# A table in a pool of its own and a new step order in a spectral mixture-of-experts kernel

## The chip, the cores and the metric

The kernel runs on one core of a Trainium2 chip. The metric is the device time of one execution in microseconds (us); the time given for a kernel is the median of its runs. Five engines work side by side, each on its own queue in order: PE (TensorE, matmuls and transposes), DVE (VectorE), ACT (ScalarE), POOL (GpSimd) and SP (SyncE). DMAs are issued from the queues of SP, ACT and POOL.

## The reference

Only what decides the computation is kept:

```python
X = np.fft.rfft(x, axis=1)                     # x: 8 x 1856 x 256
Yr = Xr @ w_r - Xi @ w_i + b_r                 # Xr, Xi: real and imaginary part
Yi = Xr @ w_i + Xi @ w_r + b_i
Yr = np.sign(Yr) * np.maximum(np.abs(Yr) - lam, 0.0)      # Yi alike, lam = 0.01
y = np.fft.irfft(Y, n=x.shape[1], axis=1)      # 14848 rows of 256
g_idx = np.argmax(y @ w_group, axis=1)         # 4 groups
e_idx = np.argmax(yg @ w_expert[g], axis=1)    # 4 experts in the group: 16 in all
h = np.maximum(ye @ w1[g, e], 0.0)             # 256 -> 1024
out[rows] = (g_w * e_w)[:, None] * (h @ w2[g, e])   # 1024 -> 256; softmax weights of both picks
```

## The kernel before

The eight sequences are worked on as four pairs. For each pair the kernel makes a Fourier transform in two stages (1856 = 58 x 32), a complex linear map with a soft threshold, and the inverse in two stages; the rows go to `ys_d` in device memory. Logits are made from the same rows, routing on DVE picks an expert for each row, and a scatter on POOL writes the row's number and weight into that expert's list `lst`. The expert layers then gather rows through these lists. Weights, rows and hidden values are split into a high and a low fp32r half, so that each product is three matmuls.

From the first pair's second stage up to the first eight expert jobs (experts 0 to 3, 256 rows each) the order of all engines' work is written out by hand. `ORDER` is a string of 1434 letters; each letter calls the next step of one generator, and a step issues its instructions to one engine at that place (`manual_schedule`). No planner changes this order afterwards. Each engine works off its own instructions in order, and waits by semaphore for what the others make. After `ORDER` the remaining experts run in a loop over `jobs`.

The letters, with the lines of the profile. A step is named below by its letter and its number from 0; with 15 steps to a pair, k45 to k59 belong to the last pair:

| letter | line | engine | what one step does |
|---|---|---|---|
| c, d | 326, 330 | PE, DVE | first stage: four 64x512 matmuls; transpose of one half |
| e | 599 | PE | second stage: matmuls with the table `T`; one step feeds two f (the eighth of a pair one) |
| f, h | 606, 611 | ACT, DVE | high and low half of a bank: `xh`, `xl` |
| j, k | 617, 627 | ACT, PE | bias into `pw`; 12 matmuls of the linear map |
| m, n, o | 637, 637, 643 | ACT, ACT, DVE | two relus and their difference: the soft threshold |
| r, s | 657, 665 | PE, DVE | inverse, first stage, four r to a pair, after the pair's last o; s is its transpose, two to an r |
| v, w, x | 676, 688, 698 | PE, ACT, DVE | inverse, second stage, eight v to a pair; w copies `ysb` and every second w issues the 512 KB store to `ys_d`; x transposes into `yt` |
| G, H | 709, 718 | PE, DVE | logits of half a pair, after the x of four v; transpose into `L` |
| R | 154 to 232 | DVE, few ACT and PE | one operation of the routing; 33 to half a pair; among them the exponentials (162, ACT), the two bf16 matmuls (208, 210, PE) and `sloti` (227) |
| S | 240 | POOL | one scatter into `lst`, 16 to half a pair |
| l | 571, 576 | SP | load of 1 MB of x, or of an expert's w1 or w2, into one of two `xt` buffers; those of experts 2 and 3 wait for the last w issued |
| W, V | 740, 745 | ACT, DVE | high and low half of 512 columns of a weight |
| I, Z | 754, 761 | SP, POOL | load of lists `ent_a`, `ent_b`; their conversion to indices |
| F | 432 | POOL | an expert job's gather: two indirect DMAs of 128 rows into `xg` |
| T, X, Y | 779, 784, 788 | PE, ACT, DVE | transposes of `xg`; high and low half |
| U, A, B | 800, 808, 812 | PE, ACT, DVE | up projection, four U to a job; relu; low half |
| D, E, J, K | 824, 836, 843, 512 | PE, ACT, DVE, POOL | down projection, four D to a job; scaling; sum; store of 128 rows |
| L, M | 857, 866 | SP, POOL | the lists for the rest, and the first gather through them |

Three things set where waits can arise. `pa` has three PSUM buffers of two banks each, for c, e, r (two buffers to a step), v, G, T, D and the routing's two matmuls; `pw` has two, one to a k. A scatter waits for the fifth one before it to have landed (the first 64 for the third, and for a matmul of an earlier step). And the gathers F0 (lists a) need `xp2`, which is opened once the last o has been issued and the forward pools are closed:

```python
if c == "o" and done == NP * 15:
    fwd.close()
    xp2 = ctx.enter_context(tc.tile_pool(name="xp2", bufs=3, side="right"))
    early["mp"] = ph.enter_context(tc.tile_pool(name="mp", bufs=1))
```

`mp` holds X's and Y's results (`xth`, `xtl`), one job's at a time.

Of the kernel before, what the change touches and what calls it, by code (L numbers as in the profile page):

```python
# [34 lines left out]


ORDER = """
jejleffhlheekkfnhmojkfnhmojcfnhkmddjocfnhkmddjocfnhcmdkdjdodcfmhcndcdjdeddcdoeddekkfnhmojkfnhmojefnhkmojkfnhmjoefnhmkojk
fnhmjoefnhmeojkkfnhmjokfnhmjokfnhmjokfnhmjorfnhmkjssorfnhmkjssornmjokssrnmjoesscffhchdvldcxwxwkddddcnmcdljcddvldxvwdwkxw
xxwdocmnvdjvdwxcxwdlGdwovxxwxvwHwxvwxexwxReRffhwhwkxRRRRRRRGRfnhmRRjoRRRRkRHRRRRRRRkfnhmjoRRnkRmRjRoRRenRmSRRojefRfehSRh  # L40
RRkRRSRRRRRSRkRfRhnmRRSojRkfRRnhSmRRRjRkfSomhnojSRrnmojSRkssSRrmRRSnRojesSseffhSRkRRhSrfmShnksjSsorSfnhmesjSscSovddkwSxx
wSvfnhvwxmSxkwxwowxSjvfnhvSwxmvxwoGwSjSkHSxxwxwRvSwxRnvxwcwSxxRcwldwkdSmdjdxSRRRcmRRRGldSdRRRoRcRnRHcjdedlddeRfRRfhhcRRo
cdkdlddRRRRefnhmRRojkRRRRRefRSRnhkmRRRRjRSoRRRkfRnShmRojRSkfRnhRmRRSRjokRfRnhSmRRRRjRRkmSonSjoRRmeRnRRjSRefofhhSkRRRSrfm
hSnksjSsorfSnhmksjSsoSrmnojSkssSrnmSojeWsWSWseffhWShvWVWvxwVwSkxwxWxwSVWvVfVlmvxSwhwkxwxSnxwojVvfSVmGhwVnSlojvSxxwkxwHSw
xRRkRmSRRnRRojRSRvmRnRvxwSxewxjowefxfhwIhkRRRRRRRRRGRfRRmZhnRjoRRHkRRRRRkfRShmnRRSojRkRmSRRnRRRSRjoReSmRnRSjoeffShRhkSRR
RRRSRRRRkRSfRmnShojRSkmnSoSRmRnSRoRSrRRFRRssrSSsSTsXSYrSUsSsrASBSUWsWSsWUASWBvAVSWBUWxSWVWDVASVwBwvSxxDwSxwVvESVvxwFxwDx
wJwlDxKVVGEJKITHvXRRYRvwZxUxwRRwFxUAxwlBURARBFRURARBDARFRRBvRRRRDxwxwRDRERJRKDRRRTERXFJRYvRUwxWxKwURRARWBTAGRFWBWRRVWVWV
WSVWUHlSRRUVRSARRBDSARRXBTSYDRRSRURERSJRRDRARRSBURRRSRRRURASDBASBUVEFWVWJDVABWlRSWDVXVSYDVEJSVDSUESWJWVUAKVWBRTARKUWBRKU
RARBKDRABXTYDRRSVVUESJDASBUSUSABDSABSUEJSDXAYSTBUSUASBDASBUESJDASBUSDSAXBDKYEJKUKUABKLDABUEJKUABMDABDDEJDKDEJKDEJK
"""  # L50
# [1151 lines left out]
```

## Time and profile before

| | |
|---|---|
| time, median of 3 runs | 1126.11 us (1124.45 to 1127.98) |
| profiled execution | 1124.21 us, its span 1122.4 us |
| DVE busy | 663.9 us (59%) |
| ACT busy | 548.5 us (49%) |
| POOL, scatters (line 240) | 128, 1021 ns of work each |
| HBM read, written | 103.49 MB, 35.00 MB |

The span is cut by time in the rows that are shown below: `ORDER` covers about 16 to 473 us of it. A row of the timeline gives start, duration, engine, line, operation, tiles and number of merged instructions, and in brackets the idle time of the engine ahead of it and what ended that. Matmuls overlap in the pipeline, so that the time of a PE step is read from its start to the start of the next one, not from its duration. PEclk is the granted clock as a share of full speed.

### The profile page before, as it was taken

The numbers are of one execution on the slowest core, as the hardware profiler recorded it, in microseconds if no ns is written. First come the engines' busy times: TensorE is split into PE (matmuls) and PEld (weight loads), VectorE is DVE, ScalarE is ACT, GpSimd is POOL, SyncE is SP. The second block draws the span as 40 slices with busy tenths as digits, with TensorE's granted clock in tenths as the row PEclk, the third lists the DMA queues.
The fourth block names the chain that finished last, engine by engine and source line by source line (L and its number), as shares of the span: only waits on it lengthen the run. The fifth ranks groups of instructions, "written<-read, shape, count | busy, mean of one in ns | idle before, by whom it ended". The sixth has DMA issues, their size and how long they took to land. (4 is left out here: it accounts for less than half of the span.)

```text
span 1122.4 us, 19716 instructions
## 1 busy us (share of the span) xinstructions
PE 1096.3 (98%) x7282; PEld 892.9 (80%) x7282; DVE 663.9 (59%) x1453; ACT 548.5 (49%) x1234; POOL 403.7 (36%) x462
## 2 busy tenths in 40 slices
PE   8999999999998999999999999999999999999996
PEld 5686576677674689899999898888979889798785
DVE  4635777686877786366647554473554745454452
ACT  2565455545653454345546544473454635444352
POOL 3000014415447567643242343323433333333311
PEclk9999999999999999999999999999999999999999
DMA  9600610360510632414424245345424354245300
GB/s 381 183 1 1 223 79 2 128 175 1 164 64 11 219 122 67 131 51 135 173 63 156 97 171 195 117 142 225 137 76 157 122 211 166 79 169 196 112 23 24
DMA packets 42500, 138.88 MB, mean 124 GB/s; under 512 B 17462, under 2 KB 19772, under 8 KB 32034
## 3 DMA queue, kind: packets, MB, share of 16 engines
q1 hardware_dynamic: 21602, 89.22, 23.1%
q0 software_dynamic: 15904, 31.48, 9.0%
q10 hardware_dynamic: 4896, 16.91, 4.1%
q8 instruction: 58, 0.95, 0.4%
q14 instruction: 40, 0.33, 0.1%
HBM read 103.49 MB, written 35.00 MB: 123 GB/s over the span
## 5 line engine op out<-in xcount | busy, mean ns | idle before, releaser
L526 PE MATMUL py<-big,hh 128*128 128x512 f32 x824 | 294.1, 398 | 0.0
L465 PE MATMUL ph<-xth,big 128*128 128x384 f32 (+1 forms) x896 | 256.3, 362 | 0.7 <-ACT xth L452 0.7
L527 PE MATMUL py<-big,hl 128*128 128x256 f32 x824 | 230.6, 280 | 0.0
L240 POOL DMA_INDIRECT lst<-ent,sloti x128 | 130.7, 1021 | 250.9 <-DVE mx_g L156 140.0
L471 DVE SCALAR_TENSOR_TENSOR hl<-ph,hh 128x256 fp32r<-128x256 f32 x448 | 151.2, 379 | 65.7 <-ACT hh L469 61.5
L526 PEld LDWEIGHTS py<-big,hh 128*128 128x128 f32 x824 | 154.8, 188 | 34.7 <-issue 3.2
L465 PEld LDWEIGHTS ph<-xth,big 128*128 128x128 f32 x896 | 165.2, 188 | 19.8 <-issue 1.5
L469 ACT ACTIVATE hh<-ph 128x256 fp32r<-128x256 f32 x448 | 134.2, 352 | 70.4 <-PE ph L465 69.8
L465 PE MATMUL ph<-xtl,big 128*128 128x384 f32 (+1 forms) x448 | 162.2, 362 | 0.3 <-DVE xtl L453 0.3
L512 POOL DMA_INDIRECT out_dram<-yo,si_f x93 | 94.6, 1017 | 178.0 <-DVE yo L534 160.0
L527 PEld LDWEIGHTS py<-big,hl 128*128 128x128 f32 x824 | 155.1, 188 | 0.1
L432 POOL DMA_INDIRECT xg<-ys_d,gi_f x93 | 90.5, 973 | 179.1 <-PE pg L448 156.3
L534 DVE SCALAR_TENSOR_TENSOR yo<-py,ent_f,yo 128x256 f32<-128x256 f32 x93 | 45.0, 484 | 163.8 <-ACT yo L533 163.8
L533 ACT ACTIVATE yo<-py,ent_f 128x256 f32<-128x256 f32 x93 | 44.1, 475 | 190.0 <-PE py L527 190.0
L415 DVE TENSOR_TENSOR big<-xt,big 128x512 fp32r<-128x512 f32 x160 | 108.9, 680 | 0.0
L414 ACT CAST big<-xt 128x512 fp32r<-128x512 f32 x160 | 99.6, 622 | 0.0
L627 PE MATMUL pw<-wh,xh 128*128 128x512 f32 x240 | 98.5, 410 | 0.0
L627 PE MATMUL pw<-wl,xh 128*128 128x512 f32 x240 | 94.8, 395 | 0.0
L465 PEld LDWEIGHTS ph<-xtl,big 128*128 128x128 f32 x448 | 84.5, 189 | 8.2 <-DVE xtl L453 0.6
L611 DVE TENSOR_TENSOR xl<-bank,xh 128x512 fp32r<-128x512 f32 x60 | 40.8, 692 | 48.2 <-PE pw L627 30.3
L599 PEld LDWEIGHTS bank<-T,big 128*128 128x128 f32 x480 | 58.5, 196 | 10.0 <-issue 3.2
L606 ACT CAST xh<-bank 128x512 fp32r<-128x512 f32 x60 | 34.2, 587 | 65.8 <-PE pw L627 56.3
(197 smaller groups left out, 1639.9 us busy)
## 6 DMA issues: line engine op xcount, KB each, us to landing
xt<-in_w_dram SPq DMA_DIRECT2D x48, 1024.0 KB, 5.1
ys_d<-ysb ACTq DMA_DIRECT2D x32, 512.0 KB, 4.8
big<-in_w_dram SPq DMA_DIRECT2D x16, 1024.0 KB, 8.7
big<-in_x_dram SPq DMA_DIRECT2D x8, 1024.0 KB, 9.7
xt<-in_x_dram SPq DMA_DIRECT2D x8, 1024.0 KB, 7.5
lst<-ent,sloti POOLq DMA_INDIRECT x128, 3.0
lst<-zero SPq DMA_DIRECT2D x1, 1920.0 KB
xg<-ys_d,gi_f POOLq DMA_INDIRECT x93, 2.8
```

The source lines that it names most:

```text
L240: ins = nc.gpsimd.indirect_dma_start(out=lst, out_offset=bass.IndirectOffsetOnAxis(ap=sl_, axis=0), in_=en_, in_offset=None, bounds_check= ...
L414: nc.scalar.copy(out=wt[:, 2 * i, cs], in_=raws[i][:, cs])
L415: nc.vector.tensor_tensor(out=wt[:, 2 * i + 1, cs], in0=raws[i][:, cs], in1=wt[:, 2 * i, cs].bitcast(F32), op=ALU.subtract)
L432: ins = nc.gpsimd.indirect_dma_start(out=xg[:, c, :], out_offset=None, in_=ys_d[0:rows, :], in_offset=bass.IndirectOffsetOnAxis(ap=ids.gi[ ...
L465: nc.tensor.matmul(o[:, :n], lhsT=a_[:, ch, fs], rhs=b_[:, ch, 0:n], start=k == 0, stop=k == 5)
L469: nc.scalar.activation(out=hh[:, f, :m], in_=ov, func=AF.Relu)
L471: nc.vector.scalar_tensor_tensor(out=hl[:, f, :m], in0=ov, scalar=0.0, in1=hh[:, f, :m].bitcast(F32), op0=ALU.max, op1=ALU.subtract)
L512: ins = nc.gpsimd.indirect_dma_start(out=out, out_offset=bass.IndirectOffsetOnAxis(ap=ids.si[:, t:t + 1], axis=0), in_=ysb, in_offset=None ...
L526: nc.tensor.matmul(o, lhsT=hh[:, f, ts], rhs=w2b[:, :, f, :], start=f == 0, stop=f == 7, skip_group_check=True)
L527: nc.tensor.matmul(o[:, 0:D], lhsT=hl[:, f, ts], rhs=w2h[:, f, :], start=False, stop=f == 7, skip_group_check=True)
L599: nc.tensor.matmul(o.rearrange("p (j c) -> p j c", j=4)[:, :, m * 32:m * 32 + 32], lhsT=zys[pr][:, k, bt, :, kp], rhs=T[:, 2 * k + kp, :], ...
L627: ins = nc.tensor.matmul(y, lhsT=a_[:, c * 128:c * 128 + 128], rhs=w_[:, c // 2, c % 2].rearrange("p j e -> p (j e)"), start=False, stop=a ...
```

## The change

The table `T` of step e moves from the pool `cf`, which lives until the last o, into a pool `ct` on the right side of SBUF, which is closed once the last e (NP * 8 = 32 of them) has been issued. `xp2` and `mp` are opened there and then, `mp` on the right side too. So a gather F and the transposes T may stand ahead of the last o. The string `ORDER` is replaced: it has the same 1434 letters, each as often as before, in another order from about the 245th on. All matmuls, copies and DMAs are the same; the code after `ORDER` is too.

```diff
-cdkdlddRRRRefnhmRRojkRRRRRefRSRnhkmRRRRjRSoRRRkfRnShmRojRSkfRnhRmRRSRjokRfRnhSmRRRRjRRkmSonSjoRRmeRnRRjSRefofhhSkRRRSrfm
+cfRnRhcmdkdjlddRRkfomhnojknmojRRneRmRojeRfRfeRRhShkRRRRSRRRRRRkfRSnhmRRRojSRkfRRnhmRRSRjRRRkRfRmShoRnRSeRjomRnRrSRfojhks
...
-    T = cf.tile([128, K1, 128], F32, name="T")
+    table_t = ExitStack()
+    ct = table_t.enter_context(tc.tile_pool(name="ct", bufs=1, side="right"))
+    T = ct.tile([128, K1, 128], F32, name="T")
...
-        done = 0
+        done, turned = 0, 0
         for c in ORDER.replace("\n", ""):
             next(steps[c])
             done += c == "o"
+            turned += c == "e"
+            if c == "e" and turned == NP * 8:
+                table_t.close()
+                xp2 = ctx.enter_context(tc.tile_pool(name="xp2", bufs=3, side="right"))
+                early["mp"] = ph.enter_context(tc.tile_pool(name="mp", bufs=1, side="right"))
             if c == "o" and done == NP * 15:
                 fwd.close()
-                xp2 = ctx.enter_context(tc.tile_pool(name="xp2", bufs=3, side="right"))
-                early["mp"] = ph.enter_context(tc.tile_pool(name="mp", bufs=1))
```

The change adds five lines ahead of or in `ORDER`'s loop, so lines from 292 on are 2 higher in the changed kernel, and those after the loop 5.

**The end of the last pair, on PE.** Before, the end of k59, the routing's second matmul (210) and two r (`x32`) follow each other, then T0, the third r and U0 (the row with `pw<-wh,xl` ends a k; 657 is r, 779 is T, 800 is U):

```order
L627 MATMUL pw<-wh,xl 128x512 x4
L210 LDWEIGHTS ones
L210 MATMUL bank<-oh,ones 128x256
L657 MATMUL bank<-big,CI 64x512 x32
L779 MATMUL bank<-K,xg 128x128 x4
L657 MATMUL bank<-big,CI 64x512 x16
L800 MATMUL ph<-xth,big 128x256
```

In the changed kernel the last e (601, four matmuls) and both matmuls of the routing stand between k58 and k59:

```order
L629 MATMUL pw<-wh,xl 128x512 x4
L601 MATMUL bank<-T,big 128x4x32 x4
L208 LDWEIGHTS sl
L208 MATMUL bank<-oh,sl 128x256
L210 LDWEIGHTS ones
L210 MATMUL bank<-oh,ones 128x256
L629 MATMUL pw<-wh,xh 128x512
```

and behind k59 comes T0 (781), then one r (659), then U0 (802):

```order
L629 MATMUL pw<-wh,xl 128x512 x4
L781 MATMUL bank<-K,xg 128x128 x4
L659 MATMUL bank<-big,CI 64x512 x16
L802 MATMUL ph<-xth,big 128x256
L802 MATMUL ph<-xtl,big 128x256
L802 MATMUL ph<-xth,big 128x256 x2
```

The last e moved from ahead of k57 to behind k58, T0 from behind two r to ahead of them, and the rows go on with r13, U1, U2, r14, U3, r15, D0, D1 and v24, so that three U more stand among the r than before.

**The gathers, on POOL.** Before, all 16 scatters of a half pair stand ahead of each of the first two gathers F0 and F1 (432), and the two stores K0 and K1 (512) behind them:

```order
L240 DMA lst<-ent,sloti 245888x2 x16
L432 DMA xg<-ys_d,gi_a 128x256 x2
L240 DMA lst<-ent,sloti 245888x2 x16
L432 DMA xg<-ys_d,gi_a 128x256 x2
L512 DMA out_dram<-yo,si_a 16384x256 x2
```

In the changed kernel:

```order
L240 DMA lst<-ent,sloti 245888x2 x9
L434 DMA xg<-ys_d,gi_a 128x256 x2
L240 DMA lst<-ent,sloti 245888x2 x21
L514 DMA out_dram<-yo,si_a 16384x256 x2
L240 DMA lst<-ent,sloti 245888x2 x2
L434 DMA xg<-ys_d,gi_a 128x256 x2
```

F0 stands behind the ninth scatter (S72) instead of the sixteenth (S79); F1 still stands behind S95, and now behind K0 and K1 too.

**The last logits, on PE and DVE.** Before, T1 (779) follows G6 (709) on PE, then v28, v29 (676), and U4 (800); G7 comes much later:

```order
L709 MATMUL bank<-yt,wg 64x256 x32
L779 MATMUL bank<-K,xg 128x128 x4
L676 MATMUL bank<-big,CI 64x256 x16
L800 MATMUL ph<-xth,big 128x256
L800 MATMUL ph<-xtl,big 128x256
```

In the changed kernel the last two v come ahead of T1 (v28 and v29 ahead of G6), and G7 follows T1 at once, ahead of U4:

```order
L711 MATMUL bank<-yt,wg 64x256 x32
L678 MATMUL bank<-big,CI 64x256 x16
L781 MATMUL bank<-K,xg 128x128 x4
L711 MATMUL bank<-yt,wg 64x256 x32
L802 MATMUL ph<-xth,big 128x256
L802 MATMUL ph<-xtl,big 128x256
```

G7 reads the last x (x63). On DVE the stretch behind H6 (718) before has Y1 (788), x (698) and R steps in turn:

```order
L718 STREAM_TRANSPOSE L<-bank 128x512
L279 SCALAR_TENSOR_TENSOR base<-K,base 128x16
L156 TENSOR_REDUCE mx_g<-L 128x16
L160 TENSOR_TENSOR ex_g<-L,mx_g 128x64
L788 TENSOR_TENSOR xtl<-bank,xth 128x512
L698 STREAM_TRANSPOSE yt<-bank 128x4x4x32 x2
```

and in the changed kernel x59 to x62 (the row of four), then the first R steps of the next routing, and x63 as the last row; 165 waits for the exponential that stands on ACT behind X1, and X1 for T1:

```order
L700 STREAM_TRANSPOSE yt<-bank 128x4x4x32 x4
L279 SCALAR_TENSOR_TENSOR base<-K,base 128x16
L156 TENSOR_REDUCE mx_g<-L 128x16
L160 TENSOR_TENSOR ex_g<-L,mx_g 128x64
L747 TENSOR_TENSOR big<-xt,big 128x512
L165 TENSOR_REDUCE sm_g<-ex_g 128x16
L168 TENSOR_TENSOR oh_g<-L,mx_g 128x64
L170 TENSOR_TENSOR oh_g<-oh_g,K 128x64
L172 TENSOR_REDUCE mx_g<-oh_g 128x16
L174 TENSOR_TENSOR oh_g<-oh_g,mx_g 128x64
L182 TENSOR_TENSOR t_3919<-L,oh_g 128x256
L700 STREAM_TRANSPOSE yt<-bank 128x4x4x32
```

On SP one weight load (576) moves ahead of the load of lists b (754); the rest of SP's order is the same. In the middle two pairs the v, c, G and e steps change places with k steps, a few letters each.

More of the change, by code (lines that the diff above doesn't have):

```diff
@@ L37 @@
 ORDER = """
[L38 to L41, printed above, removed]
@@ L42 @@
-wSvfnhvwxmSxkwxwowxSjvfnhvSwxmvxwoGwSjSkHSxxwxwRvSwxRnvxwcwSxxRcwldwkdSmdjdxSRRRcmRRRGldSdRRRoRcRnRHcjdedlddeRfRRfhhcRRo
-cdkdlddRRRRefnhmRRojkRRRRRefRSRnhkmRRRRjRSoRRRkfRnShmRojRSkfRnhRmRRSRjokRfRnhSmRRRRjRRkmSonSjoRRmeRnRRjSRefofhhSkRRRSrfm
-hSnksjSsorfSnhmksjSsoSrmnojSkssSrnmSojeWsWSWseffhWShvWVWvxwVwSkxwxWxwSVWvVfVlmvxSwhwkxwxSnxwojVvfSVmGhwVnSlojvSxxwkxwHSw
-xRRkRmSRRnRRojRSRvmRnRvxwSxewxjowefxfhwIhkRRRRRRRRRGRfRRmZhnRjoRRHkRRRRRkfRShmnRRSojRkRmSRRnRRRSRjoReSmRnRSjoeffShRhkSRR
-RRRSRRRRkRSfRmnShojRSkmnSoSRmRnSRoRSrRRFRRssrSSsSTsXSYrSUsSsrASBSUWsWSsWUASWBvAVSWBUWxSWVWDVASVwBwvSxxDwSxwVvESVvxwFxwDx
@@ L47 @@
-wJwlDxKVVGEJKITHvXRRYRvwZxUxwRRwFxUAxwlBURARBFRURARBDARFRRBvRRRRDxwxwRDRERJRKDRRRTERXFJRYvRUwxWxKwURRARWBTAGRFWBWRRVWVWV
-WSVWUHlSRRUVRSARRBDSARRXBTSYDRRSRURERSJRRDRARRSBURRRSRRRURASDBASBUVEFWVWJDVABWlRSWDVXVSYDVEJSVDSUESWJWVUAKVWBRTARKUWBRKU
-RARBKDRABXTYDRRSVVUESJDASBUSUSABDSABSUEJSDXAYSTBUSUASBDASBUESJDASBUSDSAXBDKYEJKUKUABKLDABUEJKUABMDABDDEJDKDEJKDEJK
+jejleffhlheekkfnhmojkfnhmojcfnhkmddjocfnhkmddjocfnhcmdkdjdodcfmhcndcdjdeddcdoeddekkfnhmojkfnhmojefnhkmojkfnhmojkfnhmojkf
+nhmojefnhmeojekkfnhmjokfnhmjokfnhmjokfnhmjorfnhmkjssorfnhmkjssornmjokssrnmojesscffhchdvldcxwxwkddddcnmcdljcddvldxvwdwkdw
@@ new lines @@
+xxxwocmnvdjvdwxcxwdlGdowvxxwxvwHwxvwxexwxReRffhRhkRRRRRRRwkRwxRfnhRmRRoGjfRRnhmRRRjoRRkHRRRknmjoRenRmRRjoefRfehhRkRSRRRR
+RRRRSRkRfRnhmSRRjoRkRfRnRShmRRojRkSRfRnRhmRRjSkomnSojRRmrRSnRRjoesSseffShhkRRSRRrfSmhnksjSsSorfnhmSesjskSoSrfnhSmksjsSov
+fSnhvwxmvxwSxvwowxkwxSjxwxwSwvxmGwnSojSvHxvSxwkxwRwxSxwxwRvRmSRRcwxncxwdSlGdjddSRRRRRcSHcdedldSdeRfRhfRhcRRRcddklddRRRRo
+cfRnRhcmdkdjlddRRkfomhnojknmojRRneRmRojeRfRfeRRhShkRRRRSRRRRRRkfRSnhmRRRojSRkfRRnhmRRSRjRRRkRfRmShoRnRSeRjomRnRrSRfojhks
+SsSRrfRRmhnSksjsSormSnojksSsSrmnojeSWsWWsefSfhWhvWVWvSxwVwkxwxSWxwVWvVSfVlmvxwhwkSxwxnxwoSjVGfVmhnSVjolvSHvxwvxwSxvwRwxk
@@ new lines @@
+xwSxwxRRSkRmRRRnRRjoSRweRRwxSRmRGRfRRfhnShjRoRRRkSHRRRSRkmnojIRemRnRRjoefRfhhkZRRRRSRRRRSkRfRRmhSnRojSRkfRmhSnRjoSRkRmRS
+RnRRojSRRRemRSRRnfFhRRokRRSRRRSmRRnSToXSrYSUsSsrASBSUsSsUASBrASBUSssSrABSDWsSWsWDSWVWvSVWVWvxWSVwDwxSxEDwJSwxVvESJvxwKvx
+wxvwKVwxlSwVGVSFxxwxvwHwxlvwxITxwxWRRXVRWRRRWRRwRZWxwRGRFRYRRRRRRRFRRURRRUAHFWBWRTUVWVWVAFRTABlBURRFRXDRARBYDRRSRRUVRESJ
+RRURASRBDRARSBURSRRVURSARRBDSRARRXBDSRRERJYSDRRRSUEVSVDAJlBSUSUASBRDASBUESWJWVDAKVWBRTWRKDWRXRFWRDRWWRRDYEJSVUEVSJUVAVSB
+TATVSUBVSUABSDAXBSYDSUSUASBDASBUSUSABDSXAYSDBSUKUABKDABKUKLEUJAKBEDJAKEBDJKDEJKDDEJKDMTEXJYUUAKBAUBUABDABDDEJKDEJK
```

## The prediction

> **What bounds the kernel now.** First the busy shares, then the span cut into stretches (engines' busy time, instructions; the last three numbers are the granted clock, the DMA share and GB/s):
>
> ```profile
> PE 1096.3 (98%) x7282; PEld 892.9 (80%) x7282; DVE 663.9 (59%) x1453; ACT 548.5 (49%) x1234; POOL 403.7 (36%) x462
> ...
> 16.00:326.00 310.00, 306.02 (x2473) 218.37 (x2470) 212.51 (x392) 169.34 (x294) 73.74 (x76) 1.00 0.33 109
> 326.00:346.00 20.00, 17.95 (x97) 14.55 (x103) 14.68 (x40) 12.20 (x22) 14.45 (x15) 0.99 0.02 2
> 346.00:361.00 15.00, 13.71 (x148) 5.55 (x133) 9.85 (x13) 1.53 (x3) 11.39 (x12) 0.90 0.16 19
> 361.00:406.00 45.00, 42.43 (x441) 32.46 (x440) 36.84 (x77) 25.40 (x49) 26.59 (x30) 1.00 0.56 187
> 406.00:473.00 67.00, 66.08 (x473) 61.54 (x473) 38.82 (x81) 25.21 (x48) 48.12 (x51) 1.00 0.34 96
> 473.00:1112.00 639.00, 637.55 (x3578) 555.19 (x3577) 343.14 (x838) 313.07 (x818) 224.70 (x274) 1.00 0.38 132
> ```
>
> PE is busy 98% of the span, and the change leaves every matmul in place. The last stretch isn't reordered. So only PE's waits inside the first five can be won, and new ones lost there. Next the timeline around the end of the last pair, PE's rows:
>
> ```profile
> 326.32 0.40 PE L627 MATMUL pw<-wh,xh 128*128 128x512 f32 x1
> ...
> 331.92 2.98 PE L599 MATMUL bank<-T,big 128*128 128x128 f32 x24
> ...
> 343.25 0.28 PE L210 MATMUL bank<-oh,ones 128*128 128x256 bf16 x1
> 345.59 4.49 PE L657 MATMUL bank<-big,CI 32*64 32x512 f32 x36 [2.05 <-DVE big L643]
> ...
> 358.55 1.97 PE L657 MATMUL bank<-big,CI 32*64 32x512 f32 x32
> ...
> 360.45 0.39 PE L800 MATMUL ph<-xth,big 128*128 128x256 f32 x1
> ...
> 363.38 1.13 PE L676 MATMUL bank<-big,CI 64*64 64x256 f32 x16
> ...
> 370.13 2.04 PE L676 MATMUL bank<-big,CI 64*64 64x256 f32 x32
> 372.11 0.51 PE L824 MATMUL bank<-big,hh 128*128 128x512 f32 x1
> ...
> 375.12 3.68 PE L709 MATMUL bank<-yt,wg 64*64 64x256 f32 x64
> ...
> 381.21 0.44 PE L779 MATMUL bank<-K,xg 128*128 128x128 f32 x2 [2.04 <-DMA xg<-ys_d,gi_a]
> ...
> 405.81 0.38 PE L800 MATMUL ph<-xth,big 128*128 128x256 f32 x1
> ```
>
> k55 starts at 326.32, and I count from there. The starts give the price of a step without waits: two k to 331.92, 2.80 each; e30 and e31 together about 2.7; an r 1.90 (358.55 to 360.45); a U 1.46 (two to 363.38); a v 0.99; a D 1.50 (two, 372.11 to 375.12); a G 3.6 with T1 starting at its end; a T 0.4. From k55 to 405.81, where U10 begins, 79.5 us pass. The steps in them are 5 k, e30 and e31, 4 r, 4 T, 10 U, 8 v, 8 D and 2 G: 14.0 + 2.7 + 7.6 + 1.6 + 14.6 + 7.9 + 12.0 + 7.2 = 67.6 us. So **some 12 us are lost here**, and this is what the new order reworks. Of them 7.7 lie between 343.25 and 360.45: 17.2 us for four r, a T and a U (9.5). The rest is mostly T1's wait.
>
> **The end of the pair.** The first loss starts with a wait for the last threshold:
>
> ```profile
> 343.45 0.69 ACT L637 ACTIVATE big<-pw,nlam 128x512 f32<-128x512 f32 x1 [1.66 <-PE pw L627]
> 344.04 0.68 ACT L637 ACTIVATE rn<-pw,nlam 128x512 f32<-128x512 f32 x1
> ...
> 344.75 0.69 DVE L643 TENSOR_TENSOR big<-big,rn 128x512 f32<-128x512 f32 x1
> ...
> 360.60 2.38 DVE L665 STREAM_TRANSPOSE big<-bank 128x1024 f32<-128x1024 f32 x2 [0.55 <-PE bank L657]
> ```
>
> m59, n59 and o59 take 2.3 us from k59's end to r12, with nothing on PE. Then r follows r while two transposes of 2.38 us empty the banks. The change puts T0 into the wait. T0 needs F0, so POOL counts (below): F0 lands about when o59 ends, and 1.9 us of the wait stay. Behind it the U between the r's (1.46 each, beside 2.38 on DVE) make PE's 1.90 + 1.46 as long as DVE's work, and I cost waits from r12 to D1 at 0.3 us. Lost before: 7.7; now 2.2. If the U's cover were gone, each r would again wait about a microsecond.
>
> But e31 is now behind k58. k59 needs f59, which needs m58 and n58 first; before, e30 and e31 (2.7 us) covered this, now e31 and two small matmuls (1.2) do. The three ACT operations end 2.1 us after k58 (0.2, then 0.6 each, as the rows space them): a **new wait of 1.1 us**. Net for this place: 4.4 us won.
>
> **The second gather.** T1 is what the new order cannot start earlier:
>
> ```profile
> 327.28 1.10 POOL L240 DMA_INDIRECT lst<-ent,sloti  x1 [3.82 <-DVE sloti L227]
> ...
> 348.20 1.00 POOL L432 DMA_INDIRECT xg<-ys_d,gi_a  x1 [0.30 <-issue]
> ...
> 372.33 0.98 POOL L432 DMA_INDIRECT xg<-ys_d,gi_a  x1 [0.30 <-issue]
> ...
> 383.64 0.19 POOL L254 CAST gi_b<-ent_b 128x10 int32<-128x10 f32 x1 [6.15 <-DMA ent_b<-lst]
> ...
> 385.69 1.08 POOL L432 DMA_INDIRECT xg<-ys_d,gi_b  x1 [0.65 <-issue]
> ...
> DMA to landing us min/median/max: 2.8/4.1/7.5
> ```
>
> POOL issues without a pause from S64 at 327.28 to F1 at 372.33: 34 DMAs in 45.05 us, 1.325 each. In the new order the sloti ahead of S64 stands as close behind k55, so S64 starts at about +1.2 (before +1.0). F0 is then at 1.2 + 9 x 1.325 = 13.1 and lands at 18; T0's place is there (k55 to k58 11.2, the wait, k59: 16.4). F1 has 36 DMAs ahead of it: +48.9, its second gather +50.2. By the last row it lands at +53.0 to +57.7.
>
> PE's work ahead of T1 is 14.0 (k) + 0.9 (e31) + 0.4 + 7.6 + 5.8 (U0 to U3) + 6.0 (D0 to D3) + 7.9 (v) + 3.6 = 46.2; with the 3.3 us of waits above, +49.5. So **T1 waits 3.5 to 8.2 us**; I take 5.5, T1's end at +55.4. Before it waited 2.0.
>
> **G7 right behind T1.** x63 stands behind six R steps on DVE that need the exponential on ACT, which is behind X1, which needs T1:
>
> ```profile
> 381.69 0.59 ACT L784 CAST xth<-bank 128x512 fp32r<-128x512 f32 x1 [5.99 <-PE bank L779]
> 382.17 0.26 ACT L162 ACTIVATE ex_g<-ex_g 128x64 f32<-128x64 f32 x1
> ...
> 328.97 0.22 DVE L165 TENSOR_REDUCE sm_g<-ex_g 128x16 f32<-128x64 f32 x1 [0.32 <-ACT ex_g L162]
> ...
> 330.13 0.43 DVE L182 TENSOR_TENSOR t<-L,oh_g 128x256 f32<-128x256 f32 x1
> ...
> 382.92 1.30 DVE L698 STREAM_TRANSPOSE yt<-bank 128x512 f32<-128x512 f32 x2
> ```
>
> X1 and the exponential end 0.8 us behind T1 (381.65 to 382.43), the R steps take 1.6 (328.97 to 330.56), x63 0.65, semaphores 0.2: **3.3 us of idle PE** between T1 and G7, where v28, v29 and U4 stood before. G7 starts at +58.7.
>
> **The third gather.** G7, U4 and U5 bring T2 to +65.2. F2 needs lists b, whose load waits for S95. Before, F2's first DMA was 13.4 us behind S95's end (F1's start), and its second one POOL issue (1.3) later. In the new order S95 ends at +48.9, the second DMA is at +63.6, and it lands at +66.4 to +71.1. The one wait of that chain that might shrink is the lists' landing, which fell into full queues (DMA share 0.56 on average from 361 to 406); four microseconds less would hide it all. I take T2 at +67. Then T2, U6, T3, 0.8 us more for F3, and U7, D4 to D7, U8, U9: 0.4 + 1.5 + 0.4 + 0.8 + 10.4 = 13.5. The same steps as before at 405.81 are done at +80.5; e30, done ahead of k55 in the new order, adds 1.85: **82.3 against 79.5, 2.8 us lost**, from 1.5 us won (landings at their shortest) to 7 lost.
>
> **The clock.** After the 2.05 us wait the clock was halved for one stretch, after the 2.04 us wait of T1 it was not:
>
> ```profile
> 345.60:349.00 3.40, 3.40 (x33) 1.34 (x35) 1.52 (x5) 0.00 (x0) 2.79 (x3) 0.51 0.02 1
> ...
> 381.20:384.60 3.40, 3.39 (x43) 2.35 (x44) 2.29 (x6) 1.91 (x4) 0.79 (x4) 1.00 0.37 101
> ```
>
> The first cost half of 3.4 us, and is part of the 79.5. The new waits around T1 are longer than both, so I add 1.7 us for G7 (nothing to 3.4). The 1.9 us ahead of r12, broken by T0, I cost at nothing (up to 1.7).
>
> The Trainium skill, "TensorE: Matmul & The Clock Gate", Part 1, has the clock fall only after an idle window of about 3.4 us, in windows that run free of the kernel. By that the wait ahead of r12 could cost nothing, and the sum would stay; by the first row, where 2.05 us of idle were enough, it could be 1.7 more, and the row decides.
>
> **The other stretches.** PE's waits in the first and in the fifth stretch that the moves reach:
>
> ```profile
> PE bank L326 <- DMA xt<-in_x_dram: 0.6, 1, 0.6
> ...
> PE ph L800 <- DVE hl L812: 0.9, 1, 0.9
> ```
>
> The load that c22 waits for (l7) no longer follows l6 through the queues within 5 us, since G3 now stands ahead of c18; but k38 in place of G3 covers it 0.8 us less, so I count half of the 0.6. Three k fewer are followed by another kind of step, which I estimate at 0.2 us each. I take 1.0 won, from 2.5 won to 2 lost, since many small moves there could each open a wait that no row shows. Behind U10 the 0.9 goes, as T5 and U18 no longer stand behind a low half whose weight had just landed, and small waits with it: 1.2 won. SP's one exchange, l13 ahead of the lists, costs nothing while v31, T1, G7, U4 and U5 (over 9 us of PE) lie between l13 and W20; without that cover W20 would wait for its 1 MB.
>
> **The sum.** 2.8 + 1.7 - 1.0 - 1.2 = 2.3 us lost on the profiled execution's 1124.2 (span 1122.4 and 1.8 around it): 1126.5. That execution lies 1.9 us under the median 1126.11 of the runs shown; it is one of a spread of 3.5 us, so I carry a part of this over: **1127**. A measurement of this kernel tells about 0.3% (3.4 us) from no change.
>
> **Rivals.** (1) *The gathers come in time.* If F1 lands at its shortest, the lists come four microseconds sooner and the clock stays full, the stretch wins 1.5, and with 2.5 in the others 4 us go: 1121 to 1122. For it speaks that F1's long landing fell among stores and l12; against it that POOL's 36 DMAs alone put F1 at +48.9. Chance 0.25. (2) *T1 and T2 become the bound.* In the new order v24 to v31 and with them eight 512 KB stores, l12 and l13 are closer together, right ahead of F1. Landing like the last time (7.6 us) or later, T1 ends at +58, G7 at +65, T2 waits for lists that are late too: 7 lost and two halved stretches: 1132 or so. It decides from a landing of about 6 us on. Chance 0.32. (3) *Nothing of this binds*, because PE itself comes later than POOL through waits in the first stretch that I can't see: PE's waits at T1 shrink as the new ones grow, and the sum stays within 2 us of none: 1126. It belongs with the forecast. Chance of both 0.43.
>
> **Numbers.** Forecast and (3) lie within 0.3%; (1) is faster, (2) slower. The range takes in both rivals' times and the bounds of the first stretch: 1121 to 1133.
>
> **What would show it.** Right, if PE's row of T1 (781) shows several microseconds of idle for `xg`, if G7's row (711) shows about 3 us for DVE or `yt`, and if no r waits for o by more than 2.1 nor for s. Wrong, if F1 lands ahead of +52 from k55, or if G7 starts within a microsecond of T1; then the new order wins what the r's lost.

## The result, and the profile after

The changed kernel takes **1139.45 us** (median of 4 runs, 1138.29 to 1140.81), the kernel before 1125.28 us beside it (4 runs, 1124.12 to 1127.98): a ratio of 1.0117, with an interval of 1.0096 to 1.0139. It is 14 us slower, where 1 to 2 were predicted, and outside the predicted range. Each ratio below is to the kernel before measured beside it; the runs outside the table of the experiments were taken while every kernel, the one before too, took some 70 us longer, with PE standing still for 10 us and more at a time, and of those only ratios and single rows are used.

The profiled execution has a span of 1136.5 us against 1122.4. The busy shares hardly move:

```profile
PE 1098.9 (97%) x7282; PEld 896.9 (79%) x7282; DVE 664.4 (58%) x1453; ACT 547.2 (48%) x1234; POOL 401.7 (35%) x462
```

So the 14 us are waits again. The span by stretches (columns as in the prediction, the last three the granted clock, the DMA share and GB/s):

```profile
361.00:411.00 50.00, 38.98 (x404) 29.62 (x403) 38.30 (x83) 23.50 (x46) 27.48 (x33) 0.90 0.62 185
411.00:433.70 22.70, 22.70 (x159) 20.92 (x159) 15.71 (x36) 10.30 (x20) 15.77 (x16) 1.00 0.24 54
433.70:446.40 12.70, 8.34 (x54) 7.92 (x53) 6.94 (x12) 3.49 (x7) 9.65 (x11) 0.87 0.12 32
446.40:487.00 40.60, 39.47 (x271) 36.14 (x270) 13.42 (x23) 11.26 (x21) 23.21 (x26) 1.00 0.33 98
```

PE is idle for 11 us around T1, where the prediction expected waits, and for 4.4 us in 433.70 to 446.40, where before PE was busy without a pause and nothing was expected. Both stretches have a clock below 1. PE's largest waits between 326 and 490 us, by what they waited for (us in total, times, longest):

```profile
PE bank L781 <- DMA xg<-ys_d,gi_a: 9.3, 3, 6.4
PE ph L802 <- DVE hl L814: 4.4, 1, 4.4
PE bank L711 <- DVE yt L700: 1.8, 1, 1.8
PE bank L781 <- DMA xg<-ys_d,gi_b: 1.3, 2, 0.8
```

Now PE's rows in the timeline at T0, r12, the two halves of T1, G7, U18, T7 and U28:

```profile
346.04 0.68 PE L781 MATMUL bank<-K,xg 128*128 128x128 f32 x4 [1.42 <-DMA xg<-ys_d,gi_a]
346.77 1.98 PE L659 MATMUL bank<-big,CI 32*64 32x512 f32 x32
...
386.47 0.66 PE L781 MATMUL bank<-K,xg 128*128 128x128 f32 x2 [6.43 <-DMA xg<-ys_d,gi_a]
388.60 0.69 PE L781 MATMUL bank<-K,xg 128*128 128x128 f32 x2 [1.47 <-DMA xg<-ys_d,gi_a]
389.22 5.42 PE L711 MATMUL bank<-yt,wg 64*64 64x256 f32 x64
...
440.52 0.56 PE L802 MATMUL ph<-xth,big 128*128 128x256 f32 x1 [4.36 <-DVE hl L814]
...
473.29 0.60 PE L781 MATMUL bank<-K,xg 128*128 128x128 f32 x4
474.62 0.38 PE L802 MATMUL ph<-xth,big 128*128 128x256 f32 x1 [0.73 <-ACT xth L786]
```

From such starts the span divides into pieces of equal work. In the new order e30 stands ahead of k55, and one D (1.41 us) that stood ahead of U10 stands behind it; both are allowed for:

| piece, us | before | after | difference | predicted |
|---|---|---|---|---|
| up to k55 (after: to e30) | 326.3 | 326.5 | +0.2 | -1.0 |
| from there to U10 | 79.5 | 85.3 | +5.8 | +4.5 |
| U10 to D31 | 66.0 | 73.8 | **+7.8** | **-1.2** |
| behind D31 | 650.6 | 650.9 | +0.3 | 0 |

More than half of the loss lies in a piece in which the prediction saw a small gain. Its largest wait is U18's, for the low half B16, and the rows lead back from there (POOL issues K2; ACT's row is E6 with E7; DVE's are J6 and B16):

```profile
431.58 0.98 POOL L514 DMA_INDIRECT out_dram<-yo,si_a  x1 [0.30 <-DVE xtl L790]
```

```profile
436.07 0.84 ACT L838 ACTIVATE yo<-bank,ent_b 128x256 f32<-128x256 f32 x2 [5.62 <-DMA out_dram<-yo,si_a]
```

```profile
436.58 0.48 DVE L845 SCALAR_TENSOR_TENSOR yo<-bank,ent_b,yo 128x256 f32<-128x256 f32 x1 [5.05 <-ACT yo L838]
...
439.78 0.69 DVE L814 SCALAR_TENSOR_TENSOR hl<-ph,hh 128x512 fp32r<-128x512 f32 x1
```

E6 writes an output row buffer. The pool of these, `yp`, has four, so E6 has to wait until K2 has emptied the one of E2. K2 is issued at 431.58 and its last update comes 4.4 us later. ACT stands still for 5.62 us with A16 and A17 behind E6, and on DVE B16 comes only after J6, two V, J7 and two V, whose rows lie between the two shown. In the kernel before K2 was issued at 395.32; in the new order K2 and K3 stand behind A15 and W27, 24 us after J2 had made K2's rows. POOL, the stores' order on it and the ring of four buffers were in no step of the prediction.

### The profile page after: what moved, and what is told of

It reads as the page before. It is cut to its first block, busy times and chain, and to the rows that moved or that the text cites. A ratio compares the mean times of both kernels' runs of the same rounds, so it can differ in the third digit from the quotient of the medians.

```text
span 1136.5 us, 19706 instructions
## 1 busy us (share of the span) xinstructions
PE 1098.9 (97%) x7282; PEld 896.9 (79%) x7282; DVE 664.4 (58%) x1453; ACT 547.2 (48%) x1234; POOL 401.7 (35%) x462
## 5 line engine op out<-in xcount | busy, mean ns | idle before, releaser
L608 ACT CAST xh<-bank 128x512 fp32r<-128x512 f32 x60 | 34.2, 587 | 66.1 <-PE pw L629 52.7
L629 PE MATMUL pw<-wh,xl 128*128 128x512 f32 x240 | 65.8, 396 | 0.0
```

Source lines behind the costliest of these rows:

```text
L629: ins = nc.tensor.matmul(y, lhsT=a_[:, c * 128:c * 128 + 128], rhs=w_[:, c // 2, c % 2].rearrange("p j e -> p (j e)"), start=False, stop=a ...
```

## Experiments

The theory was: about 6 us of the 7.8 come from K2 and K3 standing late (4.4 of wait, and 1.7 as the clock drops and U18 and U19 take 2.71 and 1.78 us instead of 1.42 each), and 1.9 from T7, X7 and Y7 standing right ahead of U28 without cover; the front loses its 5.8 through F1 and the full queues. The rivals: the pool itself; and that waits only hide others, so that removing one wins nothing.

The runs whose times are near the first ones, with pieces of equal work from one profiled execution of each:

| run | time, us | before beside it | ratio (interval) | e30 to U10 | U10 to D31 |
|---|---|---|---|---|---|
| before, after | 1139.45 | 1125.28 | 1.0117 (1.0096 to 1.0139) | 79.5, 85.3 | 66.0, 73.8 |
| f1_only | 1140.15 | 1125.73 | 1.0131 (1.0114 to 1.0148) | 88.2 | 73.2 |
| t2_late | 1143.51 | 1125.73 | 1.0158 (1.0141 to 1.0175) | 85.2 | 78.6 |
| l13_behind | 1135.94 | 1125.73 | 1.0093 (1.0073 to 1.0113) | 82.4 | 73.1 |
| k23_later | 1139.10 | 1125.73 | 1.0119 (1.0102 to 1.0136) | 83.9 | 74.3 |
| tail2_d | 1136.01 | 1127.40 | 1.0088 (1.0064 to 1.0112) | 83.5 | 69.0 |
| tail3 | 1131.23 | 1124.86 | 1.0058 (1.0040 to 1.0075) | 84.1 | 66.1 |

The last three have the front of the changed kernel and show 83.5 to 84.1 us there beside its 85.3: a difference of up to 1.8 us between two profiles of one front can't be read. The letters of each diff are a piece of `ORDER`.

**The pool alone** (pool_only: the order of before, `T` in its own pool, `xp2` and `mp` opened behind the last e):

```diff
-cfRnRhcmdkdjlddRRkfomhnojknmojRRneRmRojeRfRfeRRh
+cdkdlddRRRRefnhmRRojkRRRRRefRSRnhkmRRRRjRSoRRRkf
...
```

> The order of before, and the table's own pool alone. Theory (the order is all of the loss): no difference, 1125 us, within 2 us; PE's rows from k55 to U10 take the 79.5 us of before, and no T, U or r waits that did not wait there. Rival (the pool itself costs: gathers and xth now lie in the table's place, and a step that must wait for the table's last reader delays them): a wait at T0 or F0 that before did not have, 2 us or more slower.

1192.57 against 1192.76 us, ratio 1.0014 (0.9983 to 1.0045). The interval ends at 0.45%, so the pool alone can't make the 1.2% that are lost: the loss is in the order, mostly at least. A smaller cost of the pool is not excluded by this run.

**T7 and its halves ahead of U28 by six D, or 8.5 us** (t7):

```diff
-UKLEUJAKBEDJAKEBDJKDEJKDDEJKDMTEXJYUUAK
+UKLEUTJAXKBYEDJAKEBDJKDEJKDDEJKDMEJUUAK
```

> After, with T7, X7 and Y7 right behind U27 instead of right ahead of U28, so that six D steps lie between X7, Y7 and U28. Theory (U28 waits for the two halves that X7 and Y7 make of T7's transposes): the 0.7, 0.7 and 0.2 us above the usual at T7, U28 and U29 go, 1.6 us faster, 1137.8. Rival (T7's bank or gather is not free that early, or the last steps are held by the tail's stores): no change, with T7 waiting in its new place.

Ratio 1.0058 (1.0027 to 1.0090), beside 1.0093 (1.0062 to 1.0124) for the changed kernel unaltered (after_again, below): their intervals overlap. The rows tell more: T7 takes 0.36 us to the next start and U28 1.42, where the changed kernel has 1.33 and 2.13.

**The gather F1 ahead** (f1_only: F1 right behind F0, K0 and K1 in its place):

```diff
-RnRRojSRRRemRSRRnfFhRRok
+RnRRojSRRRemRSRRnfFFhRRok
...
-vESJvxwKvxwxvwKVwxlSwVGVSFxx
+vESJvxwvxwxvwVwxlSwVGVSKKxx
```

> After with F1 right behind F0 and K0, K1 in F1's old place, nothing else: as many transfers stay ahead of S95, so the lists come when they did. In the runs of after on these chips the stretch from v24 to U10 took 48.6 to 52.0 us. Theory (behind the gather stand the lists: what T1 no longer waits, T2 waits): T1's rows wait under 0.5 us for xg, and T2's or T3's wait grows by about as much, the stretch shortens by under 2 us. Rival (the gather alone holds the stretch): T1's wait goes and T2's does not grow, 3 us shorter or more.

Nothing is won. PE's rows of T1 and G7, and ACT's of the copies w60 and w61 (the two of v30):

```profile
379.95 0.63 PE L781 MATMUL bank<-K,xg 128*128 128x128 f32 x4 [0.22 <-issue]
386.67 6.67 PE L711 MATMUL bank<-yt,wg 64*64 64x256 f32 x64 [6.10 <-DVE yt L700]
```

```profile
385.19 1.07 ACT L690 COPY ysb<-bank 128x512 f32<-128x512 f32 x2 [5.61 <-DMA ys_d<-ysb]
```

T1's wait is gone, and 6.10 us of wait stand ahead of G7 instead: x needs w, and w a free `ysb`, of which there are three, each held until its 512 KB store has landed. The changed kernel has the same wait hidden beside T1's (ACT's row at 384.68: 5.00 us for `ys_d<-ysb`). So at this place there are two bounds, F1's landing and, some 2.5 us below it, the stores': G7 starts at 386.67 instead of 389.22. T2, at 397.56, waits for the lists as before. The front is no shorter for it (88.2 us), as behind G7 the rows show new losses: U6 runs on a clock of 0.50 for 3.41 us from 399.09 on, and T3 waits 1.92 us for its gather.

**l13 behind the lists** (l13_behind), as the kernel before has it:

```diff
-SFxxwxvwHwxlvwxITxwxW
+SFxxwxvwHwxvwxIlTxwxW
```

> After with the load l13 (1 MB) behind the lists' loads on SP, as before had it. Theory (that stretch is bound by what the queues carry, 1.0 of their share for 10 us: a megabyte less, 2.5 us at the 380 GB/s that it reaches there, lets the second gather and the lists land 2 us sooner): the lists' first use on POOL comes 12 us or less behind F1, T2 waits 2 us less, v24 to U10 47 us or less. Rival (the lists wait for the scatters and for their own order, not for bytes): no change, 48.6 to 52 us, and W20 may wait for l13.

Between 1 and 3 us seem won (ratio lower by 0.0024, with intervals that overlap, so the time alone doesn't show it; 83.5 to 85.3 us in the front become 82.4). PE's rows of T1, and POOL's of lists b:

```profile
386.13 0.66 PE L781 MATMUL bank<-K,xg 128*128 128x128 f32 x2 [4.94 <-ACT ysb L690]
387.74 0.69 PE L781 MATMUL bank<-K,xg 128*128 128x128 f32 x2 [0.95 <-DMA xg<-ys_d,gi_a]
```

```profile
389.81 0.19 POOL L254 CAST gi_b<-ent_b 128x10 int32<-128x10 f32 x1 [8.58 <-DMA ent_b<-lst]
```

POOL waited 12.31 us for the lists in the changed kernel, 8.58 here. One megabyte less ahead of them in the queues brings F1's second half 2.0 us sooner after its issue. The stores' bound remains: the first row names ACT's copy into `ysb`, though F1's first half landed within 0.1 us of that, so here both bounds end together.

**T2 and T3 later** (t2_late), behind D7, so that the lists have more time:

```diff
-HFWBWRTUVWVWVAFRTABlBURRFRXDRARBYDRRSRRUVRESJ
+HFWBWRUVWVWVAFRABlBURRFRDRARBDRRSRRDTXDYTUVRESJ
```

> After with T2 and T3 behind U6, U7 and D4 to D6 (D7 between them), F1, K0 and K1 as in after. The stretch from v24 to U10 then holds one D more (1.4 us). Theory (T2 waits for lists that only the transfers set, so 8.6 us of work ahead of it hide its whole wait, but T1's stays): T2's and T3's waits, 5.5 to 8.7 us on these chips, go, T1's 1.3 to 2 us and the wait ahead of G7 stay: 45.5 us with the D more. Rival (U6, U7 and the D steps wait in their turn, for ACT and DVE behind T2's halves and the new lists): 48 us or more.

A miss: slower. The front stays as long as it was, and behind it the wait of U18 grows to 6.8 us, since K2 is issued later still (438.47).

**K2 and K3, three times.** Right behind J2 and J3 (k23), in the changed kernel:

```diff
-RRUVRESJRRURAS
+RRUVRESJKRRURAS
...
-RERJYSDRRR
+RERJKYSDRRR
...
-VDAKVWBRTWRKDWRX
+VDAVWBRTWRDWRX
```

> After, with the stores K2 and K3 right behind the adds J2 and J3 that make their rows, some 20 us earlier on POOL; nothing else moves. Theory (ACT's E6 waits 5.6 us for a row buffer that K2 has not yet emptied, A16 and A17 stand behind it, so U18 waits 4.4 us and then runs on a halved clock): E6 no longer waits for out_dram, U18 starts within 0.5 us of T6, its clock stays full; 4.3 + 1.3 + 0.4 = 6.0 us faster, 1133.5. Rival (POOL is late as a whole there, by its pause of 2.7 us and one DMA per 1.29 us, so that another of its transfers holds ACT or PE instead): under 2 us faster, with the wait under another name.

Ratio 1.0116 (1.0059 to 1.0172): inconclusive. The unaltered kernel in after_again (below) has no wait of U18 for a low half either, as PE came late enough there for K2 to land in time. Still later on POOL, behind F7 (k23_later):

```diff
-VDAKVWBRTWRKDWRXRFWRD
+VDAVWBRTWRDWRXRFKKWRD
```

> After with K2 and K3 still later, behind F7 on POOL: on these chips, where PE is some 50 us later and POOL is not, K2 lands well ahead of E6 in after, and this brings back the distance that after had where it was first measured (K2 issued 4.5 us ahead of E6). Theory (E6 needs the row buffer that K2 empties, some 4.3 us from its issue; A16 and A17 stand behind E6, U18 behind them): ACT stands 3 to 5 us at E6, and U18 starts 3 us or more behind T6's end. Rival (E6 is held by its D steps or by something else on ACT): E6 starts with D15's end as in after_again, whatever K2 does.

```profile
437.20 0.47 ACT L838 ACTIVATE yo<-bank,ent_b 128x256 f32<-128x256 f32 x1 [0.76 <-DMA out_dram<-yo,si_a]
```

The time stays (1.0119). K2 is issued 1.8 us later (433.36), lands without the late update, 2.5 us on, and E6 starts as before at 435.97; the row shown is E7, waiting for K3. E6 goes with K2's last update in both kernels; what an earlier K2 does, this run doesn't show. Then **K2, K3 and T7 together** (tail2_d: the diffs of k23 and t7):

> The changed kernel with K2, K3 ahead of A15 and W27, and T7 ahead of V27, as in the kernel before. If the wait of U18 (4.4 us), its slow clock (1.6) and T7 and U28 without cover (1.6) are real losses, about 7.6 us less than the changed kernel: 1131 to 1133 us beside 1125 for the kernel before, ratio near 1.006. If they only moved slack that a later wait takes up, the ratio stays at 1.011 to 1.013.

Ratio 1.0088, between both theories: some 3 us won of 7.6 by the ratios, whose intervals overlap, and 4.8 from U10 to D31 by the rows. The rows say why. U18 no longer waits, T7 and U28 take 0.36 and 1.42 us, and a new wait stands at U29 (PE, then ACT's E8 and E12, then POOL's K4 and K8):

```profile
473.97 0.39 PE L802 MATMUL ph<-xth,big 128*128 128x256 f32 x1 [2.79 <-DVE hl L814]
```

```profile
460.08 0.47 ACT L838 ACTIVATE yo<-bank,ent_a 128x256 f32<-128x256 f32 x1 [4.48 <-DMA out_dram<-yo,si_b]
...
470.49 0.48 ACT L838 ACTIVATE yo<-bank,ent_b 128x256 f32<-128x256 f32 x1 [3.72 <-DMA out_dram<-yo,si_a]
```

```profile
457.38 0.98 POOL L514 DMA_INDIRECT out_dram<-yo,si_b  x1 [0.30 <-issue]
...
462.55 0.99 POOL L514 DMA_INDIRECT out_dram<-yo,si_a  x1 [0.30 <-DVE xtl L790]
```

It is the same ring once more: K4 to K7 stand behind the last sixteen scatters, which POOL issues without a pause, and E8 waits for K4, E12 for K8. In the kernel before K4 to K7 stand ahead of these scatters (K4 at 430.88). U18's wait had given POOL the time to catch up. So **the stores K4 to K7 ahead of the scatters** (tail3, against tail2_d):

```diff
-DYEJSVUEVSJUVAVSB
+DYEJKKKSVUEVSJKUVAVSB
...
-SUKUABKDABKUKLEUTJ
+SUUABDABULEUTJ
```

> tail2_d with the stores K4 to K7 ahead of the last sixteen scatters on POOL, where the kernel before has them, instead of behind them. In tail2_d U29 waited 2.8 us for a low half behind J12, behind E12, whose row buffer K8 had not emptied. If that wait comes from K4 to K8 standing in one burst behind the scatters (E8 4.5 us and E12 3.7 us idle on ACT), E8 and E12 no longer wait, U29 takes 1.5 us instead of 4.4, and the time is 2.5 to 3 us below tail2_d: ratio about 1.006. If K8 lands late because of the full queue alone, U29 keeps its wait and the ratio stays at 1.009.

Ratio 1.0058, as expected of the ring. ACT's E8 and E12, and PE's three largest waits between 326 and 490 us:

```profile
454.89 0.47 ACT L838 ACTIVATE yo<-bank,ent_a 128x256 f32<-128x256 f32 x1
...
464.74 0.47 ACT L838 ACTIVATE yo<-bank,ent_b 128x256 f32<-128x256 f32 x1 [2.35 <-PE bank L828]
```

```profile
PE bank L781 <- DMA xg<-ys_d,gi_a: 8.6, 3, 6.0
PE bank L711 <- DVE yt L700: 1.6, 1, 1.6
PE bank L781 <- DMA xg<-ys_d,gi_b: 0.8, 2, 0.5
```

Neither E waits for a store, no U waits for a low half, and U10 to D31 takes 66.1 us, 0.1 from the kernel before. What is left, 6.4 us by the medians, is by the rows the front: T1's wait, G6's and the lists. No run takes the front back to 79.5 us at such times, so its share is read from rows and not undone by a move.

**The good part of the change alone** (hyb_front: the order of before, in which only the piece from k59 to D0 and F0 behind S72 follow the new order, with the new pool, and F1 is moved to a place of its own, behind S84; against the order of before):

```diff
-RRSRRRRkRSfRmnShojRSkmnSoSRmRnSRoRSrRRFRRssrSSsSTsXSYrSUsSsrASBSU
+RRSFRRRRkRSfRmnShojRSmnRokRRRRRmRRnToXSrYSUsSsrASBSUsSsUASBrASBUSFss
```

> The same, and F1 behind S84, eleven scatters ahead of its place; it needs lists a alone. Theory (before's order has 8 us of work between T1 and what needs the last lists, so that an early second gather is worth what it seems to be): T1 does not wait, T2 waits under 1 us though the lists come 2.6 us later: 5 to 7 us faster than before, 1119 to 1121. Rival 1 (the stores of the second half are the bound there too: G6 or G7 waits for yt instead): 0 to 2 us faster. Rival 2 (S85 to S95, 2.6 us later, bring T2's lists too late): T2 waits 3 us or more, 2 to 4 us faster.

1190.16 us, ratio 0.9950 (0.9919 to 0.9982). With F1 left where the kernel before has it (hyb_f1old):

> The order of before, with after's arrangement of the 72 steps from k59 to D0 alone, and F0 behind S72, which the table's pool allows; F1 in before's place behind S95. Theory (after's front part wins 5 us up to v24, and T1, whose gather POOL can't issue sooner, takes them back): v24 starts 35 us behind k55 at most, counting D0 (before 38.6 with the D), T1 waits 6 us or more instead of 2.0, the whole within 2 us of before. Rival (T1's gather lands sooner, since the stores start sooner): 3 us or more faster than before.

Ratio 0.9951 (0.9932 to 0.9969). Both are faster than the kernel before, by half a per cent. No single wait could be traced to this gain, and whether 5 us of it are left at 1125 us is open.

**Runs that settled less.** The changed kernel again, unaltered (after_again):

> After once more, unchanged, as the base of the runs that edit it, since the first four runs stood beside a before of 1193 us where the earlier ones had 1125. Theory (the losses that the trace shows are in the order, whatever else the chip does): 1.2% slower than the before beside it. Rival (what slows before there covers the waits of after, or adds to them): a ratio outside 1.009 to 1.015.

Ratio 1.0093 (1.0062 to 1.0124): a loss is there too, but not the same one, as U18 does not wait for a low half. K2 and K3 late in the order of before, behind A15 and W27 (b_k23late):

> Before, with the stores K2 and K3 as late as in after (behind A15 and W27); nothing else moves. Theory (the late store alone makes the wait, in either order): E6 waits for out_dram and a U step behind it waits for hl; K2 is issued at about 427 and lands some 4 us later, E6 was due at about 426, so ACT stands 4 to 5 us and PE 3 to 4.5, with 0 to 1.7 for the clock: 1128 to 1131. Rival (the wait needs the rest of the new order, such as two V steps ahead of J7 and B16 and T5 and T6 ahead of U18): within 2 us of before, 1125.

Ratio 1.0029 (0.9998 to 1.0061): no E waits for a store in its profile, so it does not test whether late stores alone make the wait. The four moves of f1_only, t2_late, k23 and t7 at once (all4):

> After with four moves, each against one loss of its trace: F1 right behind F0, with K0 and K1 in its old place behind S95 (as many transfers stay ahead of S95); T2 and T3 behind U6, U7 and D4 to D6 (D7 between them), so that 8 us of work lie between G7 and T2; K2 and K3 right behind J2 and J3; T7, X7 and Y7 right behind U27. Theory: T1's 8.7 us of waits and G7's 1.8 us at half clock go, as its gather lands before the stores of the second half begin, and T2, whose lists stay where they are (+69.4 from k55), waits 2 us at most: 8.5 us faster; U18's 4.4 us and 1.6 of clock: 6.0; U28: 1.6. Together 16 us faster than after, 0.2% faster than before. Rival 1 (the stores and loads of that stretch are the bound, whatever gather is waited for: v29's and G7's inputs come as late as before): F1's move wins at most 2 us, 9 to 10 us faster in all, 0.5% slower than before. Rival 2 (the last lists are the bound and T2 comes later still, since K0 and K1 now stand ahead of the lists' F2): T2 waits 5 us or more, 11 us faster than after, 0.3% slower than before.

Ratio 1.0143 (1.0097 to 1.0190), a miss: the piece up to U10 got shorter by its rows, the time did not. The kernel of tail2_d three times earlier (tail2, tail2_b, tail2_c), and with l13_behind's move added (tail2_l13):

> After, with the two moves behind U10 alone: K2 and K3 right behind J2 and J3, T7, X7 and Y7 right behind U27; the stretch up to U10 as in after. Theory (the loss behind U10 is two waits: a row buffer that a late store holds, and T7 right ahead of the U that needs it): U18 and U28 wait no longer, 6.0 and 1.6 us, 7.6 us faster than after, half of what after loses against before: 0.5% slower than before. Rival (the two waits hide others of the same length): under 3 us faster, 0.9% or more slower than before.

> After, with K2 and K3 right behind J2 and J3, and T7, X7 and Y7 right behind U27; everything up to U10 as in after. Theory (what after loses behind U10 is these two waits): E6 starts with D15's end, U18 within 0.5 us of T6's end and at full clock (6.0 us), U28 without a wait (1.6): 7.6 us less than after, 1131 to 1132. Rival (POOL is late there as a whole, and holds ACT or PE elsewhere): under 3 us less.

> The changed kernel with K2, K3 ahead of A15 and W27, and T7 ahead of V27, as in the kernel before. If the wait of U18 (4.4 us), its slow clock (1.6) and T7 and U28 without cover (1.6) are real losses, about 7.6 us less than the changed kernel: 1131 to 1133 us, ratio near 1.006, with no wait of U18 for a low half above 1 us. If they only moved slack that a later wait takes up, the time stays near 1139, ratio 1.011 to 1.013.

> The same two moves, and the load l13 behind the lists' loads on SP. Theory (l13's megabyte delays the second gather and the lists by 2 to 3 us, apart from the tail): 3 us less than with the two moves alone, 1128 to 1129. Rival (what l13 won alone is the tail's wait, since with PE and POOL shifted against each other K2 landed sooner): as with the two moves alone.

Ratios 1.0040, 1.0068, 1.0065 and 1.0051: below after_again's, each with an interval of some 0.003 on either side; their profiles don't show which wait went.

## Why the prediction was wrong

- **The end of the pair: right.** 3.2 us are lost from e30 to r12 (predicted 3.0): k59 behind e31 waits, and T0 waits 1.42 us for F0 and starts at 346.04. Ahead of k59 the row names `oh` of the routing (0.59 us, at its matmul of line 208), which the prediction did not have, but f59 ends only 0.3 us later, so the predicted cause nearly coincides with it. From r12 to D1 another 0.45 are lost (0.3). Of the 7.7 us that were lost before from k59's end on, about 2 remain, T0's wait included (2.2). The four r take 1.90 us each.
- **T1: cause right, size wrong.** F1 is issued 49.6 and 50.9 us behind k55 (predicted 48.9 and 50.2). But its two halves land 8.5 and 9.4 us later, above the upper bound of 7.5 that was taken from the view of before, and T1 loses 8.75 instead of 5.5: the queues are full from the first to the last of it (DMA share 1.01 from 377.85 to 388.60). Rival (2) said this, with a time of 1132.
- **G7: wrong.** The predicted 3.3 us behind T1 aren't there: G7 starts at T1's end, as x63 is first read only past its middle, by the 19th of its 32 matmuls. What it loses is the clock, 1.85 us (5.35 from start to start instead of 3.5); 1.7 were taken.
- **The stores: missed.** f1_only shows a second bound, the three `ysb`, some 2.5 us below T1's. The prediction counted the stores only as load on the queues. G6 loses 1.83 us to them too: its x waits for the copy w54, whose `ysb` becomes free at 372.8, when v24's store, issued at 366.26, has landed.
- **SP's exchange: wrong.** "SP's one exchange, l13 ahead of the lists, costs nothing" looked at who needs l13, and not at what its megabyte does to those behind it: the lists' wait goes from 12.31 to 8.58 us without it, and the front gets 1 to 3 us shorter in the profiles, which the times alone don't show.
- **The step that failed** is "Behind U10 the 0.9 goes, as T5 and U18 no longer stand behind a low half whose weight had just landed, and small waits with it: 1.2 won". It was costed from the waits of before alone, by which moved steps they would lose; the new order's own sequence on POOL and ACT behind U10 was not followed. It held a 7.8 us loss: by the rows, K2 and K3 behind A15 and W27 keep E6, and through it U18, waiting on the ring of four (6.0 us with the clock), and T7 and U28 lose 1.9. tail3 undoes these two and the ring's next wait, and has the piece back at 66.1 us; the time falls by 0.59% of 1125, or 6.6 us, give or take some 3 by the two intervals. The split into 6.0 and 1.9 is read from rows; no run near 1125 us undid one of the two alone.
- **The first stretch** was to win 1.0 and shows +0.2 in the first profile; e30 starts between 326.3 and 328.6 us in seven kernels that share this stretch, so that one profile can't tell it from nothing.

The sum predicted 2.3 us, and 14.0 came. Of the 11.7 between them 9.0 lie behind U10.

What the waits did to the clock, in the kernel before (ahead of r12, and at T1), in the changed kernel (T0; T1 with G7; U18) and in tail2_d (T0, U29). The granted clock is the third number from the right:

```profile
342.23:345.64 3.41, 1.36 (x15) 0.79 (x14) 2.29 (x5) 1.27 (x2) 2.50 (x4) 1.00 0.02 1
345.64:349.05 3.41, 3.41 (x34) 1.35 (x36) 1.48 (x5) 0.00 (x0) 2.80 (x3) 0.50 0.02 1
...
376.37:379.78 3.41, 2.81 (x50) 1.61 (x42) 0.91 (x3) 0.00 (x0) 1.00 (x1) 1.00 0.94 327
379.78:383.19 3.41, 1.98 (x30) 1.30 (x34) 1.17 (x4) 1.14 (x3) 0.00 (x0) 1.00 0.79 272
```

```profile
345.00:348.42 3.42, 2.33 (x36) 1.00 (x36) 2.20 (x5) 1.51 (x3) 2.66 (x3) 1.00 0.14 49
...
379.14:382.55 3.41, 0.90 (x16) 0.29 (x8) 1.31 (x2) 0.53 (x2) 0.96 (x1) 1.00 1.08 365
382.55:385.96 3.41, 0.00 (x0) 0.00 (x0) 0.67 (x2) 1.07 (x2) 0.00 (x0) 0.50 0.97 226
385.96:389.38 3.42, 1.44 (x8) 0.74 (x12) 1.66 (x6) 0.67 (x2) 0.00 (x0) 0.50 0.98 395
...
437.16:440.58 3.42, 0.06 (x1) 0.06 (x1) 3.42 (x7) 0.73 (x2) 2.81 (x3) 1.00 0.12 32
440.58:443.99 3.41, 3.41 (x16) 3.41 (x17) 1.68 (x3) 0.53 (x1) 2.50 (x4) 0.50 0.02 1
```

```profile
346.33:349.74 3.41, 1.54 (x14) 0.64 (x21) 2.25 (x6) 1.62 (x3) 2.52 (x3) 1.00 0.22 53
349.74:353.15 3.41, 3.41 (x35) 1.24 (x20) 1.20 (x2) 0.23 (x1) 2.63 (x3) 0.50 0.02 1
...
469.21:472.62 3.41, 1.97 (x17) 1.76 (x15) 0.48 (x1) 0.87 (x3) 0.86 (x1) 1.00 0.49 189
472.62:476.03 3.41, 2.06 (x17) 2.06 (x18) 1.77 (x3) 1.37 (x4) 2.52 (x5) 1.00 0.25 79
```

The waits of 6.43 and 4.36 us halved the clock; those of 1.42 (T0) and 2.79 us (U29 in tail2_d) left it at 1.00. The Trainium skill, "TensorE: Matmul & The Clock Gate", Part 1, has the clock halved after an idle window of about 3.4 us. By their length these four waits agree with it. The 2.05 us wait of the kernel before, which halved the clock, still does not, if the window must be idle throughout.

The rows settle what the prediction left open, why 2.05 us cost the clock and 2.04 did not. In these traces a slow stretch lasts 3.41 us or a multiple of it (10.24 us from 382.55 on), and the windows above are counted off in steps of 3.41 us from where one starts. What PE stands idle in one of them (its length less PE's busy time) goes with the clock of the next: 2.05, 2.51, 3.41, 1.98, 3.36 and 1.87 us are each followed by 0.50, though PE was busy for part of most of these windows; the 2.04 us of T1 in the kernel before are cut by a boundary into 0.60 and 1.43, and U29's 2.79 into 1.44 and 1.35, and no window of these is followed by a lower clock. So not only the length of a wait counts, but also how it lies to the boundaries; the wait ahead of r12 cost no clock in the changed kernel (1.08 idle in the window of T0) and did cost it in tail2_d, at the same place of the same order, so that it cost nothing was partly luck. There is no sharp limit in the rows: G6's 1.83 us in the changed kernel (idle in 372.31 to 375.72) left the clock at 1.00, and what decides near there stays open.
